# Rows of q and k within SBUF, a third pair of row buffers, the memory update by 136 columns

## The chip, the cores and the metric

The kernel runs on one core of a Trainium2 chip. The metric is device time in microseconds of one execution. The kernel before took 1695.57 us (median of three runs, 1693.65 to 1700.11).

## The reference

Four layers are applied one after another to x, a matrix of 2048 rows and 512 columns: x = x + A(LN(x)), x = x + B(LN(x)), and both once more with the same weights.

A is attention with a compressive memory. The 2048 rows are cut into 4 segments of 512. There are 32 heads of 16 columns. Per head and segment:

```python
logits = qs @ ks.T * scale + causal mask;  p = softmax(logits)
a_dot  = p @ vs
a_mem  = (phi(qs) @ M) / (phi(qs) @ z + 1e-6)      # phi(t) = t + 1 where t > 0, else exp(t)
o      = g * a_mem + (1 - g) * a_dot               # g = sigmoid(beta) of the head
M += phi(ks).T @ vs;   z += sum over rows of phi(ks)
```

The result of all heads is multiplied by wo. B is a Fourier mixing: a = x @ Dre.T and b = x @ Dim.T along the 512 columns, then y = Cre @ a - Cim @ b along the 2048 rows, with given matrices.

## The kernel before, in words

All large products run on TensorE. To keep precision, most operands are split into two f16 numbers, high and low, and a product is three matmuls (high by high, high by low, low by high), collected in PSUM; this is `mm3`. A group is 8 heads of one segment (`NG` = 4 groups per segment, `NGRP` = 32 groups over two layers, numbered in order). Within a group the 8 heads are 2 halves `a` (partitions 0 to 63 and 64 to 127) of 4 heads `p`.

A group goes through these steps, each a generator in the code:

- `s_p` projects q and k of the group (transposed: head columns on partitions, 512 rows along the free axis). `t_split` makes the high and low f16 halves `hl` of each. They have to be spread so that each head's 16 columns lie on partitions of their own, in the row buffers `qst` and `kst`. For this `t_split` stores `hl` to DRAM (2 transfers, tile `d<-w`) and loads it back (4 transfers, `qst<-d` or `kst<-d`): per half, 48 partitions hold high, low, high (q) or high, high, low (k), so that one matmul over 48 partitions does all three products. Two more partitions of `kst` hold a constant (8192) that is written once by `t_ones`; two more of `qst` get the row maxima.
- `s_v` projects v into PSUM, and `t_v` writes it to `vt`. Before, a head pair has three blocks of 16 columns there: v of half 0, ones, v of half 1. So 32 neighbouring columns hold v and ones for either half, and the sums of softmax come out of the same product.
- `s_x` multiplies q by k per 128 rows and takes the maximum of each row with a mask on VectorE (tile `junk`, 32 instructions per group, row maxima `mx`); they are transposed, split and written into `qst` (`qst<-mhl`). Only one group at a time is in this step.
- `s_st` computes the transposed scores, less the maxima, and `t_sel` takes the exponential on ScalarE and the causal selection on POOL (`pt`). After its last matmul the row buffers are free (`("ST", i)`).
- `s_av` multiplies `vt` (as 128 x 32 weights, four column strips of the array) by `pt`.
- `s_mem` multiplies phi(q) by the memory `macc` (segments 1 to 3), and adds the update: phi(k) of 128 rows as weights, all of `vt` of these rows (4 x 48 = 192 columns) as the moving operand, f32, four of them per group; two products with a block mask `bd` on VectorE pick the wanted blocks.
- `s_m`, `t_merge` divide by the sums, add both parts, and split the result for `s_o`, which multiplies by wo, adds x and does the next LayerNorm.

There are `NR` = 2 pairs of row buffers (and 2 of `vt`), used in turn. Group i's rows are loaded once `("ST", i - 2)` is reached. The tile `y` (16 blocks of 512 columns) holds weights at first (`stage`; the value weights in blocks 8 to 11), then the unsplit wd and wo, and later the sums of B.

The order is not written by hand. A planner (`Plan`) steps all generators at build time: every `yield need(engine, tiles)` is a place where it chooses, by its own costs of each instruction, which generator issues next on which engine; a table `LEAN` shifts that choice per step and engine. What comes out is a fixed order on each engine and on SP's queue, from which all transfers are issued. `t_warm` adds matmuls with no use (`onesb`) where the planner expects TensorE to be idle. `tt` puts an elementwise operation on VectorE or POOL. All instructions are recorded under one line, L272, so the profile is read by tile names (`w` are working tiles, `b` PSUM banks).

Of the kernel before, what the change touches and what calls it, by code (L numbers as in the profile page):

```python
# [32 lines left out]
LEAN = dict(s_stT=150.0, s_memV=40.0, s_wV=80.0, s_rY=150.0, t_mergeA=40.0, s_xA=150.0, t_abA=40.0, t_mergeY=-150.0, s_mV=40.0, t_cV=-40.0, s_cA=-80.0, s_oY=40.0, t_cY=80.0, t_lnG=80.0, t_splitV=-40.0, t_phiA=150.0, s_kV=-300.0, t_mergeV=150.0, s_cT=80.0, s_avT=80.0, s_wA=-150.0, t_resV=-150.0, t_selG=40.0, s_lnY=-150.0, t_rowsY=300.0, t_ktY=-80.0)  # L33
# [9 lines left out]
PHM, EARLYLN, FEW = 5, 1, 0  # L43
WARM, IDLE, SPARE = 4200, 500.0, 300.0
DEEP = 1500.0
AHEAD = 2
NR = 2


class Plan:  # L50
# [31 lines left out]
    def key(self, a):  # L82
        f = self.fine.get(a.tensor.name)
        return (a.tensor.name, a.offset // f) if f else a.tensor.name
# [70 lines left out]
    def op(self, eng, name, args, kw):  # L155
# [123 lines left out]
def body(ctx: ExitStack, tc: tile.TileContext, x, wq, wk, wv, wo, beta, wd, cs, out):  # L279
# [61 lines left out]
    vt = [const.tile([128, TT, NP, 3, 16], F32, name=f"vt{i}") for i in range(NR)]  # L341
# [5 lines left out]
    bd = const.tile([128, 2, 4, 32], F32, name="bd")  # L347
# [65 lines left out]
    def share(o, src, s):  # L413
        yield need("A", src, s)
        A.activation(o[:, 0], src, AF.Copy, scale=s)
        A.activation(src, src, AF.Copy, scale=s)
        yield need("VG", o, src)
        tt(o[:, 1], src, o[:, 0], OP.subtract)

# [105 lines left out]
    def t_ones():  # L525
        yield need("G", tag="mz")
        c8 = sb("mz", F16, (32, 128))
        G.memset(c8, 8192.0)
        d8 = tc.dram_tile([2, 2048], F16, name="d8")
        yield gate(("dk", 0))  # L530
        yield need("Y", c8, mode="b")
        Y.dma_start(d8.rearrange("o (p n) -> (o p) n", n=128), c8, est=(609, 341, 172))
        pl.close(c8)
        for i in range(NR):
            for a in range(2):
                yield need("Y", d8, mode="b")
                Y.dma_start(kst[i][64 * a + 48:64 * a + 50].rearrange("r p n -> r (p n)"), d8, est=(415, 341, 472))
        done.add("KR")

    def s_k():  # L540
# [12 lines left out]
        for j in range(NR):  # L553
            V.memset(vt[j][:, :, :, 1, :], 1.0)
        done.add("VI")
        yield need("V")
        bits(rp, 3, 1.0)
        bits(ra, 64, 1.0 / 64)
        cj = sb("en", F32, (128, 2, 4, 32))
# [25 lines left out]
    def t_ln(src, xi, dst, key, direct=False):  # L585
        st = rg("bst", 2, F32, (128, 6))
        V.bn_stats(st, src)
        mv = rg("mv", 6, F32, (128, 4))
        V.bn_aggr(mv[:, 0:2], st)
        yield need("G", mv)  # L590
        rs = rg("rs", 6, F32, (128, 1))
        G.tensor_scalar(mv[:, 2:3], mv[:, 1:2], 1e-5, 2.0 ** -20, op0=OP.add, op1=OP.mult)
        G.tensor_tensor(rs, mv[:, 2:3], mhalf, op=OP.pow)
        G.tensor_scalar(mv[:, 3:4], mv[:, 0:1], rs, -1.0, op0=OP.mult, op1=OP.mult)
# [6 lines left out]
        else:  # L601
            A.activation(hl[:, 0], xi, AF.Copy)
        yield need("VG", xi, hl)
        tt(hl[:, 1], xi, hl[:, 0], OP.subtract)
        pl.close(xi)
        if direct:
# [7 lines left out]
            if pl.free["A"] <= pl.free["V"]:  # L614
# [36 lines left out]
    def t_merge(e, o, gi, g, n, key):  # L651
# [7 lines left out]
        rc = rg("rc", 4, F32, (128, 2, 16))  # L659
        xa = x[:, 0]  # L660

        def view(off, *dims):
            return bass.AP(xa.tensor, xa.offset + off, [list(xa.ap[0])] + [list(d) for d in dims])

        yield need("V", x)
        d = view(16, (496, 2), (32, 16))
        if not gi:
            V.tensor_scalar(rc, d, 1e-6, None, op0=OP.add)
            d = rc
# [4 lines left out]
        for a in range(2):  # L674
            c = slice(16 * a, 16 * a + 16)
            tt(n.rearrange("p (b r) -> p b r", r=32)[:, :, c], view(528 * a, (32, 16), (1, 16)),
# [4 lines left out]
    def t_split(p, key, f, kphi):  # L681
# [10 lines left out]
        done.add(("half", key))  # L692
        yield need("Y", hl)
        d = tc.dram_tile([2, 2, 64, 512], F16)
        for a in range(2):
            Y.dma_start(d[a].rearrange("j p n -> p j n"), hl[64 * a:64 * a + 64], est=(651, 702, 467))
        i = key[1]
        if not kphi or q:
            pl.close(hl)
        elif i >= NR:  # L700
            spawn(t_kt(hl, kphi))
        if i >= NR:
            yield gate(("ST", i - NR))
        yield need("Y", d)
        order = key[0] == "dq"
        dst = (qst if order else kst)[i % NR]
        for a in range(2):
            f = d[a].rearrange("j (d p) n -> (j d) (p n)", p=NP)
            o = dst[64 * a:64 * a + 64].rearrange("r p n -> r (p n)")
            if order:  # L710
# [6 lines left out]
        if kphi and not q and i < NR:  # L717
            yield from t_kt(hl, kphi)
# [41 lines left out]
    def t_v(p, i):  # L760
        yield need("A", p)
        A.activation(vt[i % NR].rearrange("p t j e d -> p (t j) e d")[:, :, 0:3:2, :],
                     p.rearrange("p t (j e d) -> p (t j) e d", j=NP, e=2), AF.Copy, scale=2.0 ** -24)
# [74 lines left out]
    def s_mem():  # L838
        for i in range(NGRP):
# [14 lines left out]
            if s < NSEG - 1:  # L854
# [10 lines left out]
                for a in range(2):  # L865
                    V.tensor_tensor(mu[:, a], mp[:, :, 16 * a:16 * a + 32], bd[:, a], op=OP.mult)
# [28 lines left out]
    def s_x():  # L895
        for i in range(NGRP):
            yield gate(("dq", i), ("dk", i), "CM")
            qs, ks = qst[i % NR], kst[i % NR]
            mx = rg("mx", 2, F32, (128, 2, NP, TT))
# [20 lines left out]
            mhl = rg("mhl", 2, F16, (32, 2, 128))  # L920
# [25 lines left out]
    def s_st():  # L946
        for i in range(NGRP):
            yield gate(("X", i), "KR")
            qs, ks = qst[i % NR], kst[i % NR]
# [143 lines left out]
    def t_c(i, raw, sc, cc):  # L1093
        A.activation(cc[:, 0], raw, AF.Copy, scale=sc)
        A.activation(raw, raw, AF.Copy, scale=sc)
# [8 lines left out]
    def s_c():  # L1104
        k = u = 0
        while u < nunit:
# [18 lines left out]
            gi = gv.bitcast(I32)  # L1125
            V.tensor_scalar(gi, gi, 0x7F800000, None, op0=OP.bitwise_and)
            V.tensor_scalar(csc[:, :m].bitcast(I32), gi, -1.0, float(268 << 23), op0=OP.mult, op1=OP.add)
# [200 lines left out]
```

## Time and profile before

| | |
|---|---|
| runs | 1693.65, 1695.57, 1700.11 us |
| profiled execution | 1699.92 us, its span 1698.2 us |
| mean granted TensorE clock | 0.989 of full speed |
| busy | TensorE 1662.3 us, VectorE 1036.8, ScalarE 872.3, POOL 810.3 |
| matmuls | 11145 records; an f32 matmul leaves two |
| DMA | 222.92 MB, 131 GB/s in the mean |

PE stands for TensorE's matmuls, PEld for its weight loads, DVE for VectorE, ACT for ScalarE, POOL for GpSimd, SPq for the queue of transfers on SyncE. A row of a group shows the operation, the tiles written and read, the size and count, then busy us, the mean ns of one, and the idle time of the engine before them with what ended it. Mean durations of pipelined matmuls overlap; busy time divided by count is what one holds of the engine. In a row of a timeline the first two numbers are start and length in us, and xN is how many instructions are merged.

### The profile page before, as it was taken

How to read it: one execution, taken by the hardware profiler on the slowest of the kernel's cores; microseconds unless marked ns; L12 is line 12 of the kernel's file. 1: busy time of each engine (PE TensorE's matmuls, PEld its weight loads, DVE VectorE, ACT ScalarE, POOL GpSimd, SP SyncE). 2: the span in 40 equal slices, each digit the busy share in tenths (PEclk: the TensorE clock that was granted, in tenths of full speed). 3: DMA queues.
4: the chain of work that ended last, by engine and by line, in shares of the span. 5: the costliest groups of instructions: out<-in, count | busy, mean ns of one | idle time of the engine just before them, and what ended most of it. 6: DMA issues, size and time to landing. Idle time of an engine off the chain costs nothing.

```text
span 1698.2 us, 32247 instructions
## 1 busy us (share of the span) xinstructions
PE 1662.3 (98%) x11145; PEld 734.7 (43%) x11145; DVE 1036.8 (61%) x3262; ACT 872.3 (51%) x1480; POOL 810.3 (48%) x1445
## 2 busy tenths in 40 slices
PE   8889999999999999999999999999999999999999
PEld 4344344444444344444544444443444444444444
DVE  8784865778677786635768558546575765433221
ACT  5487577755656666535376754655455325312000
POOL 4376556575565556634255644635454415322000
PEclk9789999999999999999999999999999999999999
DMA  7546545655357432525746663543435322131423
GB/s 182 147 116 178 128 132 159 172 142 152 94 148 208 126 119 84 189 56 196 193 148 187 182 179 90 132 116 98 140 91 149 105 85 76 57 125 38 143 70 123
DMA packets 208629, 222.92 MB, mean 131 GB/s; under 512 B 104520, under 2 KB 127048, under 8 KB 208464
## 3 DMA queue, kind: packets, MB, share of 16 engines
q1 hardware_dynamic: 208464, 220.85, 45.8%
q8 instruction: 88, 1.44, 0.4%
q14 instruction: 77, 0.63, 0.1%
HBM read 137.40 MB, written 61.87 MB: 117 GB/s over the span
## 4 chain that ended last, share of the span: by engine, by line
PE 77%; DVE 9%; ACT 5%; issue 4%; DMA 3%; POOL 2%; SPq 1%; ACTq 0%; DVEq 0%; POOLq 0%
PE b L272 77%; ACT w L272 4%; DVE junk L272 4%; SPq L272 1%; DVE w L272 1%; POOL w L272 1%; DMA w<-w 1%; DMA w<-x 1%; DVE m L272 1%; DVE mx L272 1%; DVE y L272 1%; DVE bst L272 0%; DVE cam L272 0%; DMA w<-in_cs_dram 0%; DVE pmax L272 0%
## 5 line engine op out<-in xcount | busy, mean ns | idle before, releaser
L272 PEld LDWEIGHTS <-w 128*128 128x128 f16 x5056 | 467.8, 98 | 612.8 <-issue 101.1
L272 PE MATMUL b<-w,w 128*128 128x512 f16 x3072 | 708.5, 380 | 1.7 <-DVE mx L272 0.8
L272 ACT ACTIVATE w<-b,fac 128x512 f32<-128x512 f32 (+1 forms) x728 | 419.2, 655 | 176.3 <-PE b L272 175.8
L272 DVE CUSTOM_DVE_ANT_0 junk<-b,cmask 128x128 bf16<-128x128 f32 (+3 forms) x1024 | 436.3, 483 | 71.6 <-PE b L272 71.1
L272 POOL TENSOR_TENSOR w<-w,w 128x512 f16<-128x512 f32 (+1 forms) x294 | 347.5, 1187 | 247.1 <-ACT w L272 223.6
L272 POOL TENSOR_SCALAR_AFFINE_SELECT w<-w 128x128 f32<-128x128 f32 (+2 forms) x704 | 237.0, 350 | 202.7 <-ACT w L272 194.1
L272 DVE SCALAR_TENSOR_TENSOR y<-b,fyu,y 128x512 f32<-128x512 f32 x200 | 148.9, 745 | 235.6 <-PE b L272 235.2
L272 ACT ACTIVATE w<-w,csc 128x512 f16<-128x512 f32 (+1 forms) x256 | 180.1, 720 | 41.5 <-DVE csc L272 32.8
L272 PE MATMUL b<-g,w 128*128 128x512 f16 x768 | 183.1, 383 | 3.2 <-DMA g<-w 0.8
L272 PE MATMUL b<-wd,w 128*128 128x512 f16 x768 | 176.8, 379 | 0.1
L272 PE MATMUL b<-w,vt 128*32 128x512 f32 (+3 forms) x2048 | 172.4, 449 | 1.9 <-POOL w L272 1.1
L272 ACT ACTIVATE w<-b 128x512 f16<-128x512 f32 x128 | 75.9, 596 | 189.4 <-PE b L272 179.3
L272 DVE SCALAR_TENSOR_TENSOR w<-b,w 128x512 f16<-128x512 f32 x128 | 87.6, 687 | 120.3 <-ACT w L272 118.7
L272 ACT ACTIVATE w<-w 128x512 f16<-128x512 f32 (+1 forms) x137 | 86.5, 632 | 90.1 <-DVE w L272 87.9
L272 PE MATMUL b<-kst,qst 48*128 48x128 f16 (+3 forms) x1024 | 117.5, 304 | 6.3 <-DVE mx L272 3.2
L272 PE MATMUL b<-qst,kst 50*128 50x512 f16 (+3 forms) x1024 | 115.8, 302 | 5.5 <-DVE mx L272 2.2
L272 PE MATMUL b<-w,g 128*128 128x128 f16 x1536 | 96.3, 221 | 0.0
L272 PEld LDWEIGHTS <-g 128*128 128x128 f16 x1536 | 89.6, 99 | 12.7 <-issue 7.8
L272 DVE STREAM_TRANSPOSE m<-b 128x512 f32<-128x512 f32 x112 | 75.6, 698 | 31.1 <-PE b L272 30.7
L272 PEld LDWEIGHTS b<-w,vt 128*32 128x32 f32 x2048 | 54.8, 110 | 87.7 <-issue 48.2
L272 PE MATMUL b<-wo,w 128*128 128x512 f16 x384 | 89.1, 379 | 0.0
L272 PEld LDWEIGHTS <-kst 50*128 50x128 f16 x1024 | 37.3, 94 | 111.7 <-issue 105.2
(105 smaller groups left out, 1019.3 us busy)
## 6 DMA issues: line engine op xcount, KB each, us to landing
w<-in_cs_dram SPq DMA_DIRECT2D x128, 256.0 KB, 3.5
cc<-w SPq DMA_DIRECT2D x128, 256.0 KB, 3.2
w<-cc SPq DMA_DIRECT2D x128, 256.0 KB, 3.1
w<-w SPq DMA_DIRECT2D x96, 256.0 KB, 3.5
d<-w SPq DMA_DIRECT2D x128, 128.0 KB, 2.5
w<-in_x_dram SPq DMA_DIRECT2D x32, 256.0 KB, 3.6
qst<-d SPq DMA_DIRECT2D x64, 128.0 KB, 2.7
kst<-d SPq DMA_DIRECT2D x64, 128.0 KB, 3.3
```

The lines of the kernel that those rows point to most:

```text
L272: r = f(*args, **kw)
```

## The change

- A third pair of row buffers, `kst[2]` and `qst[2]`, is laid over blocks 8 to 11 of y, as f16. Group 2 alone uses it (`ring`); its rows wait until the four value weights have been split (`("W", 2, g)`). Groups from 3 on alternate between pairs 0 and 1; group 3 now waits for group 0, group 4 for group 1, and from group 5 on each for the group two before it, as earlier (`prior`).
- Where the buffer is free when a transfer is planned (groups 0 to 2, and others whose predecessor's step is already planned), `t_split` writes the rows with six transfers from `hl` straight into the row buffer. Otherwise it goes through DRAM as before.
- `vt` is laid out as 16 columns of v and 16 of ones, each with the 8 heads innermost; the host orders the columns of wv so. The update multiplies by the first 17 x 8 = 136 columns; the second attention product takes as weights 32 columns that lie 8 apart. `bd` becomes bf16, and the two products on VectorE read other slices.
- Added waiting points (`YL`, `YB`, `YM`, `YC`, `YS`, all 1) let the planner put other instructions between dependent ones. In the LayerNorms of each layer's first segment (`direct`), two small operations and the low half's subtraction move from POOL to VectorE (`STARTV`); there ScalarE empties PSUM only if it is ahead of VectorE by 300 ns.
- Planner costs for some ScalarE and POOL instructions change, the warming matmuls no longer wait for the mask, and the table `LEAN` has new values. `mx` and `mhl` have one buffer instead of two, `rc` two instead of four. The number of junk tiles stays two.

```diff
-LEAN = dict(s_stT=150.0, ..., t_abA=40.0, ..., s_oY=40.0, t_cY=80.0, t_lnG=80.0, ..., s_cT=80.0, ..., t_ktY=-80.0)
+LEAN = dict(s_stT=150.0, ..., t_abA=150.0, ..., t_cY=80.0, t_lnG=-300.0, ..., s_cT=150.0, ..., s_ldY=300.0, t_lnA=80.0, t_lnY=-40.0, t_abV=300.0, s_oY=40.0, s_oT=150.0, t_phkV=80.0)
+STARTV, YL, YB, YM, YC, YS = 1, 1, 1, 1, 1, 1
+DIRECT = 3
...
+            if name == "activation" and isinstance(kw.get("bias"), bass.AP):
+                c += 80
...
+            if n <= 32:
+                lat = 172
             if name == "tensor_tensor" and kw.get("op") == OP.pow:
-                c = 300 + n * 165
+                c = 290 + n * 165
...
-    vt = [const.tile([128, TT, NP, 3, 16], F32, name=f"vt{i}") for i in range(NR)]
+    kst.append(y[:, 8:10, :].bitcast(F16).rearrange("p a (b n) -> p (a b) n", n=512))
+    qst.append(y[:, 10:12, :].bitcast(F16).rearrange("p a (b n) -> p (a b) n", n=512))
+    ring = [0, 1, 2] + [(i - 3) % 2 for i in range(3, NGRP)]
+    prior = [None] * 3 + [0, 1] + list(range(3, NGRP - 2))
+    vt = [const.tile([128, TT, 32, HG], F32, name=f"vt{i}") for i in range(NR)]
...
-            V.memset(vt[j][:, :, :, 1, :], 1.0)
+            V.memset(vt[j][:, :, 16:, :], 1.0)
...
@@ t_split @@
+        i = key[1]
+        keep = kphi and not q
+        dst = (qst if q else kst)[ring[i]]
         yield need("Y", hl)
+        if i < DIRECT or prior[i] is not None and ("ST", prior[i]) in done:
+            if i == NR:
+                yield gate(*[("W", 2, g) for g in range(NG)])
+            for a in range(2):
+                o = dst[64 * a:64 * a + 64]
+                for r, j in ((0, 0), (16, 1), (32, 0)) if q else ((0, 0), (16, 0), (32, 1)):
+                    yield need("Y", hl)
+                    Y.dma_start(o[r:r + 16], hl[64 * a:64 * a + 64, j], est=(415, 520, 800))
+            done.add(key)
...
+            return
         d = tc.dram_tile([2, 2, 64, 512], F16)
...
-        if i >= NR:
-            yield gate(("ST", i - NR))
+        if i > NR:
+            yield gate(("ST", prior[i]))
...
@@ s_mem @@
-                mp = ps("pj", F32, (128, NP, 48))
+                mp = ps("pj", F32, (128, 17, HG))
                 for t in range(TT):
-                    T.matmul(mp, phk[:, 128 * t:128 * t + 128], v[:, t], start=(t == 0), stop=(t == TT - 1))
+                    T.matmul(mp, phk[:, 128 * t:128 * t + 128], v[:, t, :17], start=(t == 0), stop=(t == TT - 1))
...
-                for a in range(2):
-                    V.tensor_tensor(mu[:, a], mp[:, :, 16 * a:16 * a + 32], bd[:, a], op=OP.mult)
+                for e, d in ((0, HG), (16, 0)):
+                    V.tensor_tensor(view(mu, e, (128, 2), (32, NP), (1, 16)),
+                                    view(mp, HG * e, (NP, 2), (1, NP), (d, 16)),
+                                    view(bd, e, (128, 2), (32, NP), (1, 16)), op=OP.mult)
...
@@ s_av @@
-                                 v[:, t, p].rearrange("k e d -> k (e d)")[:, 16 * a:16 * a + 32], tiles[p][1],
+                                 v[:, t, :, NP * a + p], tiles[p][1],
...
@@ t_ln @@
+        if direct and STARTV:
+            yield need("V", mv)
+            V.tensor_scalar(mv[:, 2:3], mv[:, 1:2], 1e-5, 2.0 ** -20, op0=OP.add, op1=OP.mult)
+            yield need("G", mv)
+            G.tensor_tensor(rs, mv[:, 2:3], mhalf, op=OP.pow)
+            yield need("V", mv, rs)
+            V.tensor_scalar(mv[:, 3:4], mv[:, 0:1], rs, -1.0, op0=OP.mult, op1=OP.mult)
...
-        if "CM" not in done or at - pl.free["T"] < IDLE or pl.lately(at) >= WARM:
+        if at - pl.free["T"] < IDLE or pl.lately(at) >= WARM:
...
-        "wv": f["A_wv"],
+        "wv": f["A_wv"].reshape(D, NG, NP, 2, DH).transpose(0, 1, 4, 3, 2).reshape(D, D),
```

More of the change, by code (lines that the diff above doesn't have):

```diff
@@ L418, in share, with view @@
         tt(o[:, 1], src, o[:, 0], OP.subtract)
+    def view(t, off, *dims):
+        return bass.AP(t.tensor, t.offset + off, [list(t.ap[0])] + [list(d) for d in dims])
     def flat(t):
@@ L601, in t_ln @@
         else:
+            if YL:
+                yield need("A", xi)
             A.activation(hl[:, 0], xi, AF.Copy)
-        yield need("VG", xi, hl)
-        tt(hl[:, 1], xi, hl[:, 0], OP.subtract)
+        if direct:
+            yield need("V", xi, hl)
+            V.tensor_tensor(hl[:, 1], xi, hl[:, 0], op=OP.subtract)
+        else:
+            yield need("VG", xi, hl)
+            tt(hl[:, 1], xi, hl[:, 0], OP.subtract)
         pl.close(xi)
@@ L658, in t_merge @@
         pl.close(e, o)
[L659 to L663, printed above, removed]
+        rc = rg("rc", 2, F32, (128, 2, 16))
         yield need("V", x)
-        d = view(16, (496, 2), (32, 16))
+        d = view(x, 16, (512, 2), (32, 16))
         if not gi:
             V.tensor_scalar(rc, d, 1e-6, None, op0=OP.add)
+            if YM:
+                yield need("V", rc)
             d = rc
@@ L692, in t_split @@
         done.add(("half", key))
+        i = key[1]
+        keep = kphi and not q
+        dst = (qst if q else kst)[ring[i]]
         yield need("Y", hl)
+        if i < DIRECT or prior[i] is not None and ("ST", prior[i]) in done:
+            if i == NR:
+                yield gate(*[("W", 2, g) for g in range(NG)])
+            for a in range(2):
[4 more added lines that the diff above has]
+            done.add(key)
+            if keep:
+                yield from t_kt(hl, kphi)
+            else:
+                pl.close(hl)
+            return
         d = tc.dram_tile([2, 2, 64, 512], F16)
@@ L696, in t_split @@
             Y.dma_start(d[a].rearrange("j p n -> p j n"), hl[64 * a:64 * a + 64], est=(651, 702, 467))
-        i = key[1]
-        if not kphi or q:
+        if keep:
+            spawn(t_kt(hl, kphi))
+        else:
             pl.close(hl)
-        elif i >= NR:
-            spawn(t_kt(hl, kphi))
-        if i >= NR:
-            yield gate(("ST", i - NR))
+        if i > NR:
+            yield gate(("ST", prior[i]))
         yield need("Y", d)
-        order = key[0] == "dq"
-        dst = (qst if order else kst)[i % NR]
         for a in range(2):
@@ L897, in s_x @@
             yield gate(("dq", i), ("dk", i), "CM")
[L898 to L899 removed]
+            qs, ks = qst[ring[i]], kst[ring[i]]
+            mx = rg("mx", 1, F32, (128, 2, NP, TT))
             left = [0]
@@ L947, in s_st @@
         for i in range(NGRP):
-            yield gate(("X", i), "KR")
-            qs, ks = qst[i % NR], kst[i % NR]
+            yield gate(("X", i), ("KR", ring[i]))
+            qs, ks = qst[ring[i]], kst[ring[i]]
             kt = scores("t")
```

51 lines of the change are left out of this document (34 added, 17 removed).

## The prediction

> **What bounds the kernel now.** I read the page first: span, busy time by engine and the chain that ended last.
>
> ```profile
> span 1698.2 us, 32247 instructions
> ...
> PE 1662.3 (98%) x11145; PEld 734.7 (43%) x11145; DVE 1036.8 (61%) x3262; ACT 872.3 (51%) x1480; POOL 810.3 (48%) x1445
> ...
> PE 77%; DVE 9%; ACT 5%; issue 4%; DMA 3%; POOL 2%; SPq 1%; ACTq 0%; DVEq 0%; POOLq 0%
> ```
>
> TensorE is busy for 98% of the span and holds 77% of the chain; only 1698.2 - 1662.3 = 35.9 us are free of it. But a busy matmul may be a slow one, so the second view was the busy time by stretch. Its columns are the stretch, its length, busy us of each engine with the instructions begun, and the granted clock.
>
> ```profile
> core 0: us, PE busy (x) PEld busy (x) DVE busy (x) ACT busy (x) POOL busy (x), PEclk, DMA share, GB/s
> ...
> 20.00:40.00 20.00, 19.50 (x176) 11.29 (x174) 18.38 (x73) 13.79 (x24) 8.10 (x7) 1.00 0.58 145
> 40.00:60.00 20.00, 16.59 (x82) 5.84 (x81) 20.00 (x81) 6.73 (x12) 6.16 (x7) 0.94 0.84 253
> 60.00:70.00 10.00, 8.18 (x29) 2.02 (x28) 9.18 (x32) 5.23 (x10) 3.11 (x11) 0.50 0.01 2
> 70.00:80.00 10.00, 9.79 (x42) 3.09 (x42) 3.23 (x11) 4.61 (x10) 3.66 (x6) 0.76 0.46 107
> 80.00:90.00 10.00, 9.86 (x120) 6.39 (x120) 5.16 (x18) 9.12 (x17) 8.29 (x16) 1.00 0.76 146
> 90.00:100.00 10.00, 8.79 (x73) 3.69 (x74) 8.04 (x42) 9.97 (x20) 8.40 (x19) 0.94 0.64 173
> 100.00:120.00 20.00, 17.85 (x157) 9.18 (x148) 16.92 (x74) 14.56 (x25) 14.86 (x25) 0.78 0.40 107
> 120.00:140.00 20.00, 17.44 (x122) 5.24 (x122) 11.56 (x37) 18.39 (x34) 14.42 (x31) 0.83 0.27 70
> 140.00:160.00 20.00, 19.57 (x150) 8.11 (x150) 6.46 (x12) 18.22 (x33) 13.72 (x27) 1.00 0.78 223
> ...
> 200.00:700.00 500.00, 496.38 (x3520) 214.77 (x3519) 352.24 (x1084) 325.45 (x553) 303.65 (x525) 1.00 0.49 138
> 700.00:900.00 200.00, 196.41 (x1211) 91.24 (x1210) 116.36 (x343) 105.23 (x168) 90.83 (x129) 0.99 0.54 161
> 900.00:1500.00 600.00, 595.12 (x4245) 260.98 (x4243) 367.99 (x1207) 300.35 (x525) 289.64 (x571) 1.00 0.43 117
> ...
> 1600.00:1650.00 50.00, 50.00 (x233) 22.70 (x232) 12.02 (x16) 0.00 (x0) 0.00 (x0) 1.00 0.34 116
> ```
>
> There are two regimes. From 200 us on TensorE sets the pace: 496 of 500 and 595 of 600 us. Between 40 and 140 us it does not: few matmuls begin, and the clock falls to 0.50 in one stretch and 0.76 to 0.83 in others. There the attention of the first four groups sets the pace, one after another, since nothing else is ready before the first segment's output exists. The third view asks where the row maxima of the scores (32 per group, on VectorE, tile junk) lie; the fourth takes the row transfers of the third group, numbered 2, from the timeline of SP's queue, beside the last score matmuls of group 0 and the last split of a value weight.
>
> ```profile
> core 0: us, DVE busy (x), PEclk, DMA share, GB/s
> 34.00:50.00 16.00, 13.28 (x32) 1.00 0.94 255
> 50.00:70.00 20.00, 13.63 (x32) 0.69 0.33 115
> 70.00:90.00 20.00, 0.00 (x0) 0.88 0.61 127
> 90.00:110.00 20.00, 13.48 (x32) 0.80 0.53 133
> ```
>
> ```profile
> 72.97 2.63 SPq L272 DMA_DIRECT2D d<-w  x4
> ...
> 83.43 1.74 SPq L272 DMA_DIRECT2D qst<-d  x4
> 85.21 1.81 SPq L272 DMA_DIRECT2D kst<-d  x4
> ```
>
> ```profile
> 83.01 0.40 PE L272 MATMUL b<-qst,kst 50*128 50x128 f16 x8
> ```
>
> ```profile
> 59.01 1.16 POOL L272 TENSOR_TENSOR w<-y,w 128x512 f16<-128x512 f32 x1 [0.21 <-ACT y L272]
> ```
>
> Groups 0 and 1 take their maxima until 70 us, then none is taken for 20 us, and group 2 follows from 90. Its rows were stored to DRAM by 72.97 + 2.63 = 75.6 us, but loaded only at 83.43, the moment the last matmul on group 0's buffers ended (83.01 + 0.40 = 83.41). So one hole at the start is a wait for a buffer.
>
> **The change, part by part.** *Third pair of row buffers.* Group 2 gets rows of its own, in a part of y that held the value weights; they are free once the last value weight is split, at 59.01 + 1.16 = 60.2 us, well before 73. The load need no longer wait for 83.41. With q and k split at 73, twelve issues at the 2.63 / 4 = 0.66 us of the store row make 7.9 us at most, and with a landing the maxima of group 2 can start at 79 to 83 instead of 90. Group 3, which waited for group 1's buffers, now waits for group 0's, so it follows group 2 directly. From group 5 on the buffer waited for is the same as before. The new wait of group 2's rows on the value weights' split sits on SP's queue; the next segment's inputs and the transposes for its LayerNorm stand behind it there, and they are wanted only when the projections of segment 1 begin. What can be won is bounded by nothing at all (ScalarE, 14.56 + 18.39 + 18.22 = 51.2 of 60 us busy from 100 to 160, paces the rest anyway) and by the whole hole of 20 us. I take what VectorE was idle in the hole, 6.8 us of 70:80 and 4.8 us of 80:90, together -12 us (0 to -20). What is late next is ScalarE's exponentials.
>
> *Direct transfers.* Where the buffer is free when the transfer is planned, the two stores and four loads of a q or k become six transfers within SBUF; the issues on SP's queue stay six. In steady state a group's rows wait for a buffer, as group 2's did, so the old way stays and nothing is won. Groups 0 to 2 and the first of layer 2 profit.
>
> ```profile
> d<-w SPq DMA_DIRECT2D x128, 128.0 KB, 2.5
> ...
> kst<-d SPq DMA_DIRECT2D x64, 128.0 KB, 3.3
> ...
> qst<-mhl SPq DMA_DIRECT2D x128, 4.0 KB, 1.7
> ```
>
> The store and the load took 2.5 + 3.3 us to land. A transfer within SBUF of 64 KB is not in the trace: the one of 4 KB took 1.7 us, and I let it cost up to the 3.3 of the load. That saves 2.5 to 4.1 us of latency. At group 0 VectorE has only 20 - 18.38 = 1.6 us free in 20:40 to use it: -1.5 us (0 to -3). At layer 2's start TensorE is idle for 200 - 196.41 = 3.6 us in 700:900: -1 us (0 to -2.5).
>
> *Update by 136 columns.* The memory update multiplies phi(k) with 17 x 8 = 136 columns of values and ones in place of 192.
>
> ```profile
> L272 PE MATMUL b<-w,g 128*128 128x128 f16 x1536 | 96.3, 221 | 0.0
> L272 PEld LDWEIGHTS <-g 128*128 128x128 f16 x1536 | 89.6, 99 | 12.7 <-issue 7.8 <-DVE fac L272 0.2
> ...
> L272 PE MATMUL b<-vt,w 128*128 128x192 f32 x192 | 38.6, 338 | 1.4 <-ACT vt L272 1.2 <-POOL w L272 0.2
> ...
> L272 PEld LDWEIGHTS b<-vt,w 128*128 128x128 f32 x192 | 30.9, 190 | 10.7 <-issue 2.7 <-DVE mx L272 2.3 <-ACT vt L272 1.6
> ```
>
> 192 records hold TensorE for 38.6 us. If all of it goes with the columns, 38.6 x 56 / 192 = 11.3 us are saved; if the weight load of 190 ns binds, nothing. In the nearest row, the projections of v, loads of 99 ns stand before matmuls that hold TensorE for 96.3 / 1536 = 63 ns each, so a load longer than its matmul is mostly hidden; I take -8 us (0 to -11). They lie on TensorE, which is the bound in most of the span. VectorE's two products per update keep their count and size.
>
> *Values with the head innermost.* The price of that is the weight of the second attention product: 32 values side by side become 32 values eight apart.
>
> ```profile
> L272 PEld LDWEIGHTS b<-w,vt 128*32 128x32 f32 x2048 | 54.8, 110 | 87.7 <-issue 48.2 <-POOL w L272 23.4 <-DVE mx L272 3.0
> ```
>
> ```profile
> L272 PE MATMUL b<-w,vt 128*32 128x128 f32 x512 | 21.4, 280 | 0.7 <-POOL w L272 0.5
> ```
>
> No load of the trace is strided. Four loads go side by side, so 2048 make 512 passes. Lower end: no cost. Upper end: the strided 32 columns cost what 128 do in one row, 190 in place of 110 ns, and all 80 ns of every pass are exposed: 512 x 0.08 = 41 us. Since the loads are issued ahead of matmuls of 280 ns and more, I take it close to the lower end: 27 ns (a third of the 80) exposed in the 128 passes of the shortest matmuls, 3.5 us, rounded to +3. [...]
>
> *The rest.* The added waiting points and the planner's new costs issue no instruction, and one buffer less for mx, mhl and rc binds nothing, because the next group's scores are planned after the transpose that reads mx. Should it bind, VectorE's maxima would queue behind it. In the first LayerNorms a subtraction and two small operations per tile move from POOL to VectorE; VectorE has 1.6 us free there, so I count 0 (1.5 either way). The new table reorders everything and I cannot derive its order. Its reach: the matmuls with 512 f16 columns.
>
> ```profile
> L272 PE MATMUL b<-w,w 128*128 128x512 f16 x3072 | 708.5, 380 | 1.7 <-DVE mx L272 0.8 <-ACT w L272 0.4
> ...
> L272 PE MATMUL b<-g,w 128*128 128x512 f16 x768 | 183.1, 383 | 3.2 <-DMA g<-w 0.8 <-ACT w L272 0.7 <-ACT g L272 0.7
> ...
> L272 PE MATMUL b<-wd,w 128*128 128x512 f16 x768 | 176.8, 379 | 0.1
> ...
> L272 PE MATMUL b<-wo,w 128*128 128x512 f16 x384 | 89.1, 379 | 0.0
> ```
>
> They hold TensorE for 1157.5 us; at the pace of 1600:1650, 50 / 233 = 0.2146 us each, the 4992 would take 1071 us. A table can move some of these 86 us, either way. I count 0 in the sum and 17 us (a fifth, my choice) as a rival in each direction.
>
> **The sum.** -12 - 1.5 - 1 - 8 + 3 = -19.5 us. The profiled execution took 1699.92 us, its span and 1.7 us around it, so 1680.4; it lies 4.35 us above the median of 1695.57, so against the median the forecast is 1676 us.
>
> **The rivals.** *ScalarE paces the start anyway.* For it: 51.2 of 60 us busy from 100 to 160, and 9.97 of 10 in 90:100. Against: 5.2, 4.6 of 10 us in the stretches before, where the earlier work would go. The start is then worth nothing, only -8 + 3 remain: 1691 us. The same comes out if the third pair does not do what it says, because the planner still sends group 2's rows late.
>
> *The table fills the gaps, or opens them.* 17 us less than the forecast is 1659; 17 us more, 1693. For it: 86 us of gaps. Against: TensorE waits visibly only 3.6 of 500 us from 200 to 700, so no single wait can be named that it removes.
>
> *The strided weights stall TensorE: slower.* Place: every pass of the second attention product, where the load stands between two matmuls of the same array columns. The price is the full 41 us in place of 3: 1676 + 38 = 1714. It decides from (19.5 + 3) / 512 = 44 ns exposed per pass, where it eats the whole gain. Against: four loads run beside each other, and 54.8 us busy for 2048 loads of 110 ns says that most of a load is latency that overlaps.
>
> **How the numbers follow.** Forecast 0.55, ScalarE or an idle third pair 0.18, a better table 0.13, a worse one 0.06, strided weights 0.08. The likeliest case alone spans 1660 to 1690: the start from 0 to -20 and the update from 0 to -11, not both at an end. The range 1655 to 1699 takes in all but the last case and half of the tail of the better table. About 0.5%, 8.5 us, is what a measurement of this kernel tells from no change. Faster by more, under 1687: nearly all of the forecast, the better table and a part of the second case, 0.72. Within: most of the second case and the worse table, 0.18. Slower: the strided weights and a little of the worse table, 0.10.
>
> **What would show it.** In the changed kernel's windows the 32 maxima of group 2 begin before 84 us, and those of group 3 before 105. The row b<-vt,w has 136 columns and under 33 us. The load row b<-w,vt stays near 110 ns and the busy time of its matmuls of 128 columns near 21.4 us; 190 ns and twice the busy time would mean the slower case. Stretches after 200 us hold as many matmuls per us as now, or the table has moved them. The prediction is wrong if the clock in 40:140 stays as low with the hole closed, for then the start was not paced by buffers.

## The result and the profile after

The changed kernel takes 1719.47 us (median of four runs, 1711.94 to 1720.61) against 1696.17 us of the kernel before on the same chip: a ratio of 1.0127, with a 95% interval of 1.0111 to 1.0143. It is slower by 23 us; the forecast was 1676 us, and the time lies beyond the range. The profiled execution took 1719.67 us.

The page of the changed kernel, with its span, busy times, shares of the chain and two rows of the transfers:

```profile
span 1717.9 us, 32388 instructions
...
PE 1664.3 (97%) x11160; PEld 742.7 (43%) x11160; DVE 1042.8 (61%) x3290; ACT 862.8 (50%) x1478; POOL 796.9 (46%) x1419
...
PE 77%; DVE 8%; issue 4%; DMA 4%; ACT 3%; POOL 2%; SPq 2%; DVEq 0%; ACTq 0%; POOLq 0%
...
kst<-w SPq DMA_DIRECT2D x120, 64.0 KB, 2.6
qst<-w SPq DMA_DIRECT2D x108, 64.0 KB, 2.9
```

Nothing here looks like a new bound. TensorE is still 97% busy and the chain has nearly the same shares. What changed is small in every line: TensorE is idle for 1717.9 - 1664.3 = 53.6 us in place of 35.9. That is 17.7 of the 19.7 us by which the span grew. The last two rows hold the surprise, to which we come below.

Where the idle time lies is told by the stretches of the changed kernel:

```profile
core 0: us, PE busy (x) PEld busy (x) DVE busy (x) ACT busy (x) POOL busy (x), PEclk, DMA share, GB/s
0.00:200.00 200.00, 171.17 (x1231) 77.39 (x1235) 145.28 (x533) 125.39 (x214) 104.05 (x193) 0.90 0.47 132
200.00:700.00 500.00, 490.40 (x3502) 214.45 (x3495) 352.69 (x1115) 318.07 (x546) 297.31 (x516) 1.00 0.45 128
700.00:1500.00 800.00, 788.46 (x5441) 353.93 (x5440) 487.87 (x1560) 401.94 (x691) 371.18 (x678) 1.00 0.43 125
```

The two stretches of the kernel before that the prediction does not show in this form:

```profile
0.00:200.00 200.00, 180.08 (x1276) 79.88 (x1276) 153.10 (x564) 129.49 (x219) 114.00 (x205) 0.91 0.58 155
...
700.00:1500.00 800.00, 791.52 (x5454) 352.22 (x5453) 484.35 (x1549) 405.58 (x691) 380.47 (x700) 1.00 0.46 128
```

TensorE's idle time in the three stretches is 28.8, 9.6 and 11.5 us after, against 19.9, 3.6 and 8.5 us before. So half of the added idle time arises in the first 200 us, which the change was expected to shorten, and half in the steady part, where the prediction expected a gain.

The maxima of the changed kernel (tile junk), by stretches cut at the groups:

```profile
core 0: us, DVE busy (x), PEclk, DMA share, GB/s
34.00:49.00 15.00, 0.02 (x1) 1.00 0.45 121
49.00:69.00 20.00, 13.62 (x32) 0.83 0.71 227
69.00:93.00 24.00, 13.75 (x32) 0.86 0.51 138
93.00:98.00 5.00, 0.00 (x0) 1.00 0.92 218
98.00:115.00 17.00, 13.49 (x32) 0.90 0.34 103
```

The hole of some 20 us between groups 1 and 2 is down to about 6 us, so the third pair does what it was said to do. But group 0 begins at 49 us, where it began at 35 us before, group 1 at 72 where it began at 51, and group 2 at 98.6 where it began at 91.

The products that use the values, by shape, in the changed kernel:

```profile
L280 PE MATMUL b<-vt,w 128*128 128x136 f32 x192 | 28.9, 290 | 3.0 <-ACT vt L280 0.9 <-DVE m L280 0.8 <-POOL w L280 0.8
...
L280 PE MATMUL b<-w,vt 128*32 128x128 f32 x512 | 22.9, 287 | 1.0 <-POOL w L280 0.7
```

```profile
L280 PEld LDWEIGHTS b<-w,vt 128*32 128x32 f32 x2048 | 67.7, 145 | 82.7 <-issue 47.8
```

The update holds TensorE for 28.9 us in place of 38.6, and a strided load takes 145 ns in place of 110. TensorE's busy time as a whole is 2.0 us longer all the same; among what grew are the warming matmuls (tile onesb), 28.4 us against 23.5.

### The profile page after: what moved, and what is told of

It reads as the page before. It is cut to its first block, busy times and chain, and to the rows that moved or that the text cites. A ratio compares the mean times of both kernels' runs of the same rounds, so it can differ in the third digit from the quotient of the medians.

```text
span 1717.9 us, 32388 instructions
## 1 busy us (share of the span) xinstructions
PE 1664.3 (97%) x11160; PEld 742.7 (43%) x11160; DVE 1042.8 (61%) x3290; ACT 862.8 (50%) x1478; POOL 796.9 (46%) x1419
## 4 chain that ended last, share of the span: by engine, by line
PE 77%; DVE 8%; issue 4%; DMA 4%; ACT 3%; POOL 2%; SPq 2%; DVEq 0%; ACTq 0%; POOLq 0%
PE b L280 77%; DVE junk L280 3%; ACT w L280 3%; DMA w<-w 2%; SPq L280 2%; POOL w L280 2%; DVE w L280 1%; DVE mx L280 1%; DMA w<-in_x_dram 1%; DVE m L280 0%; DVE y L280 0%; DVE cam L280 0%; DVE bst L280 0%; DVE pmax L280 0%; DMA qst<-w 0%
## 5 line engine op out<-in xcount | busy, mean ns | idle before, releaser
L280 POOL TENSOR_TENSOR w<-w,w 128x512 f16<-128x512 f32 (+1 forms) x285 | 336.4, 1188 | 189.7 <-ACT w L280 175.9
L280 ACT ACTIVATE w<-w,csc 128x512 f16<-128x512 f32 (+1 forms) x256 | 174.2, 725 | 29.1 <-DVE csc L280 25.1
L280 PE MATMUL b<-qst,kst 50*128 50x512 f16 (+1 forms) x992 | 112.7, 301 | 11.4 <-ACT w L280 5.9
L280 PE MATMUL b<-kst,qst 48*128 48x128 f16 (+1 forms) x992 | 111.1, 302 | 5.5 <-DVE mx L280 2.9
L280 PEld LDWEIGHTS b<-w,vt 128*32 128x32 f32 x2048 | 67.7, 145 | 82.7 <-issue 47.8
L280 DVE TENSOR_REDUCE cam<-w 128x1 bf16<-128x512 f32 x128 | 82.0, 677 | 16.9 <-DMA w<-in_cs_dram 16.6
L280 DVE STREAM_TRANSPOSE m<-b 128x512 f32<-128x512 f32 x112 | 76.2, 699 | 19.9 <-PE b L280 17.4
```

Of the source, the lines that this page charges most:

```text
L280: r = f(*args, **kw)
```

## The experiments

The question was which part costs the time. Five theories stood: the new order by itself (O), the strided weights (W), the direct transfers' time on SP's queue (D), the late start by the waiting points (S), and the bytes of the direct transfers (B).

**The parts alone, in the order of before.** The first kernel takes only the layout with the head innermost (with the bf16 mask and the fewer buffers for mx, mhl and rc), the second also the 136 columns, both with every queue's order as it was.

```diff
 s1_stride
+    vt = [const.tile([128, TT, 32, HG], F32, name=f"vt{i}") for i in range(NR)]
+    T.matmul(mp, phk[:, 128 * t:128 * t + 128], v[:, t, :24], ...)      # still 192 columns
+    v[:, t, :, NP * a + p]                                              # strided weights of s_av
+    "wv": f["A_wv"].reshape(D, NG, NP, 2, DH).transpose(0, 1, 4, 3, 2).reshape(D, D),
 s2_update, on top of it
-    T.matmul(mp, ..., v[:, t, :24], ...)
+    T.matmul(mp[:, :17], ..., v[:, t, :17], ...)                        # 136 columns
```

> The kernel before with its order of instructions on every engine kept, and only the layout of the values changed: head innermost, so the second attention product loads weights 8 apart; the memory update still multiplies 192 columns. Theory O (the order): the loss of the changed kernel lies in the new order of the work and not in its edits, so this one costs 0 to 5 us over the kernel before; the load row rises from 110 to about 145 ns and the excess of these matmuls by some 4 us. Theory W (strided weights, the rival of the prediction): 20 us or more over the kernel before. Theory D (direct row transfers): as O, 0 to 5 us.

> As s1_stride, same order of instructions, and the update multiplies 136 columns. O: the row of the update falls from 38.6 to about 29 us as in the changed kernel, so 10 us less than s1_stride, 5 to 10 us under the kernel before. W: still 10 us or more over the kernel before. D: as O.

The layout alone takes 1698.59 us against 1696.72, a ratio of 1.0012 (1.0003 to 1.0022); with 136 columns 1695.75 us, 0.9996 (0.9986 to 1.0005). The weight loads of the first, and the update of the second:

```profile
L273 PEld LDWEIGHTS b<-w,vt 128*32 128x32 f32 x2048 | 69.3, 144 | 79.0 <-issue 45.7 <-POOL w L273 21.5 <-DVE mx L273 2.4
```

```profile
L273 PE MATMUL b<-vt,w 128*128 128x136 f32 x192 | 29.6, 291 | 1.2 <-ACT vt L273 1.0
```

2048 loads, each 34 ns longer, cost 2 us (0.5 to 3.7 by the interval): W falls as the cause of 23 us. The narrower update frees 38.6 - 29.6 = 9.0 us of TensorE's busy time, yet the kernel gains only 1698.59 - 1695.75 = 2.8 us. The span falls by no more, 1695.7 to 1693.2 us, and the other rows of matmuls became 5.7 us longer together, 4.6 of them in the scores (tiles qst and kst); the granted clock was 0.990 in the mean of the profiled execution, against 0.993. Why they became longer was not followed. An engine that is 98% busy did not hand on here all that was taken off it.

**The direct transfers alone, in the order of before.**

```diff
 s3_direct, in t_split
+        if i < NR or ("ST", i - NR) in done:
+            six  Y.dma_start(o[r:r + 16], hl[64 * a:64 * a + 64, j])   # where the stores stood
+        else:
             the two stores, and later the four loads
```

> The kernel before with its order kept, and rows of q and k moved within SBUF at the place of the store wherever the buffer is planned to be free then (two pairs of buffers, not three). O: within 3 us of the kernel before, since what waits for the rows keeps its place in every queue. W: no difference. D: each direct transfer holds the queue of SP for 0.59 us where a load took 0.43, and what stands behind is late: 10 to 20 us over the kernel before.

1732.60 us, a ratio of 1.0207 (1.0193 to 1.0221). The direction is D's, but 36 us are more than it had said, and where the rest arises was not followed. SP's queue in this kernel, around 275 us:

```profile
272.47 3.86 SPq L273 DMA_DIRECT2D qst<-w  x6
276.44 3.74 SPq L273 DMA_DIRECT2D kst<-w  x6
280.62 1.29 SPq L273 DMA_TRANSPOSE w<-w  x1
```

The same place in the kernel before:

```profile
268.94 2.73 SPq L272 DMA_DIRECT2D d<-w  x4
271.76 1.31 SPq L272 DMA_TRANSPOSE w<-w  x1
```

The DMA_TRANSPOSE turns k for phi(k). Before, four stores of 2.73 us together stood ahead of it; the loads came later, behind it. Now twelve transfers of 3.86 + 3.74 = 7.6 us stand ahead of it, and it is issued 8.15 us after the first of them in place of 2.82, so 5.3 us later. The rows of 36 of the 64 sets (a set is a q or a k of one group) reach their buffer without DRAM, and the kernel loses.

**Parts taken out of the changed kernel, its order kept.** In s4 the values have their old layout and the update its 192 columns. In s5 only two of a q's or k's six direct transfers are issued from group 3 on, and in s9 all six with half of the columns each; these two leave rows stale, so they tell of time alone.

```diff
 s4_oldvalues
+    vt = [const.tile([128, TT, NP, 3, 16], F32, name=f"vt{i}") for i in range(NR)]
+    T.matmul(mp, ..., v[:, t], ...)                                     # 192 columns, contiguous weights
 s5_third
+    if i < DIRECT or r == 0:
         Y.dma_start(o[r:r + 16], hl[64 * a:64 * a + 64, j], ...)
 s9_half
+    if i < DIRECT:
         Y.dma_start(o[r:r + 16], hl[64 * a:64 * a + 64, j], ...)
+    else:
+        Y.dma_start(o[r:r + 16, :, :256], hl[64 * a:64 * a + 64, j, :256], ...)
```

> The changed kernel with its order kept, and the old layout of the values and the update by 192 columns put back. O: the update's 10 us come back and the strided loads' 4 us go: 1723 to 1728 us, slower than the changed kernel. W: 1690 to 1700 us, as the stall goes. D: as O.

1717.36 us, 1.0123 (1.0105 to 1.0141): 2 us less than the changed kernel, where O and D had expected more time and W 1690 to 1700 us. In the new order the two edits on the values together are worth nothing, or cost 2 us. The loads are back at 110 ns.

> The changed kernel with its order kept; of the six direct transfers of a q or k only two are issued from group 3 on, so the other rows keep what an earlier group left there (the scores of these groups are computed from rows that are partly old; all other work is the same). It takes 0.59 us of SP's queue per transfer left out. Theory D (the issue time of the direct transfers makes SP's queue late, and all that stands behind it): 1700 to 1710 us, 10 to 20 us less than the changed kernel. Theory O (the new order itself, with whatever transfers): 1717 to 1720 us.

1703.75 us, 1.0052 (1.0033 to 1.0071): without two thirds of these transfers about 16 of the 23 us are gone, as D had said.

> The changed kernel with its order kept and every transfer still issued, but from group 3 on each direct transfer moves only half of its columns (the other half of the rows stays from an earlier group; nothing else is left out). Theory D in its narrow form (what costs is the time that SP's queue needs to issue 12 transfers before the transpose of k behind them): 1716 to 1721 us, as the changed kernel. Rival B (the bytes, that is the landing of the rows or the load on the DMA engines): 1706 to 1713 us, half or more of the way to s5_third's 1703.75.

1721.58 us, 1.0154 (1.0139 to 1.0169), level with the changed kernel. Its issues of k's rows, and the landing of those with half the bytes:

```profile
L281 SPq DMA_DIRECT2D kst<-w x120: 546/591/652, 38.9 to 1321.9; - x120
```

```profile
kst<-w SPq DMA_DIRECT2D x108, 32.0 KB, 2.0
```

Half the bytes land in 2.0 us in place of 2.6, and the kernel gains nothing; an issue still takes 591 ns in the median. So B falls, and with it a late landing of the rows: what counts is the number of issues. What one issue costs, from the tile kst of the changed kernel (count, then shortest, median and longest in ns):

```profile
L280 SPq DMA_DIRECT2D kst<-w x120: 546/592/1077, 39.0 to 1319.4; - x120
L280 SPq DMA_DIRECT2D kst<-d x48: 245/418/966, 63.8 to 1416.0; - x48
```

A direct transfer holds SP's queue for 592 ns, a load from DRAM for 418. The planner counts 415 for either, so the twelve of a q and a k are through 12 x 0.18 = 2.1 us later than it believes. (s5 takes out eight of the twelve, 4.7 us, and so more than this error: its 16 us are no measure of the wrong price alone.) The chain from there to TensorE can be followed at one place. SP's queue of the changed kernel:

```profile
1065.20 1.93 SPq L280 DMA_DIRECT2D qst<-w  x3
1067.18 0.57 SPq L280 DMA_DIRECT2D w<-w  x1
1067.85 1.82 SPq L280 DMA_DIRECT2D qst<-w  x3
1069.72 3.80 SPq L280 DMA_DIRECT2D kst<-w  x6
1073.61 1.27 SPq L280 DMA_TRANSPOSE w<-w  x1
```

The same instructions in s5, with a third of the transfers:

```profile
1050.53 0.60 SPq L280 DMA_DIRECT2D qst<-w  x1
1051.18 0.58 SPq L280 DMA_DIRECT2D w<-w  x1
1051.85 0.59 SPq L280 DMA_DIRECT2D qst<-w  x1
1052.49 1.23 SPq L280 DMA_DIRECT2D kst<-w  x2
1053.83 2.45 SPq L280 DMA_TRANSPOSE w<-w  x1
```

From the first of q to the transpose it is 8.4 us in the one and 3.3 us in the other. Then, in the changed kernel, the timelines of POOL, ScalarE and TensorE, one row each:

```profile
1076.78 1.15 POOL L280 TENSOR_TENSOR w<-w 128x512 f32<-128x512 f16 x1 [3.79 <-DMA w<-w]
```

```profile
1077.97 0.72 ACT L280 ACTIVATE w<-w,fac 128x512 f32<-128x512 f32 x1 [4.85 <-POOL w L280]
```

```profile
1080.88 0.79 PE L280 MATMUL b<-qst,kst 50*128 50x384 f16 x3 [1.35 <-ACT w L280]
```

POOL adds the halves of k when the transposed k lands, ScalarE waits 4.85 us to begin phi(k), and the exponentials that are to empty PSUM stand behind phi(k) in ScalarE's fixed order. So the score matmuls find no free bank and TensorE waits 1.35 us. In s5, ScalarE's wait at the same instruction is this:

```profile
1060.51 0.72 ACT L280 ACTIVATE w<-w,fac 128x512 f32<-128x512 f32 x1 [1.03 <-POOL w L280]
```

One such place costs TensorE 1.5 us at most in the changed kernel, the longest wait of the second row below, and no page shows it as a bound. TensorE's waits for ScalarE's working tiles over the whole kernel (sum, count, longest) before, after, and in s5:

```profile
PE b L272 <- ACT w L272: 5.1, 13, 0.9
```

```profile
PE b L280 <- ACT w L280: 12.6, 23, 1.5
```

```profile
PE b L280 <- ACT w L280: 8.3, 17, 1.6
```

So this wait is 7.5 of the 17.7 us of added idle time, and 4.3 of the 9.2 us of idle time that s5 takes away (53.6 - 44.4). Most of the rest of what s5 wins lies in TensorE's waits for VectorE (mx from 10.3 to 7.7 us, w from 4.8 to 1.8), which were not followed back to the queue. Nor does a late ScalarE cost time by itself: it stands idle ahead of this step of phi(k) for 37.3 us in the changed kernel, 14.8 before and 19.2 in s5, but also for 34.9 us in s11 below, the fastest kernel of all, whose TensorE waits for it for 1.2 us at most. At the place above it costs, since the next matmuls of TensorE stand behind it. No run moved the transpose alone in the changed kernel's order.

The stretches of s5 show which part of the loss the transfers make:

```profile
0.00:200.00 200.00, 170.54 (x1235) 76.96 (x1239) 145.66 (x534) 125.49 (x214) 104.73 (x193) 0.91 0.46 131
200.00:700.00 500.00, 494.91 (x3533) 217.80 (x3526) 356.28 (x1123) 321.52 (x552) 302.22 (x521) 1.00 0.43 124
700.00:1500.00 800.00, 794.04 (x5485) 357.17 (x5484) 493.24 (x1565) 403.82 (x694) 376.94 (x687) 1.00 0.41 118
```

TensorE idles 5.1 and 6.0 us in the steady stretches, where it was 9.6 and 11.5, and 3.6 and 8.5 before. The idle time added in the steady part is that of the transfers. The first 200 us still have 29.5 us of idle time: that half has another cause.

**Parts taken out, the planner ordering anew.** In these the order of everything changes with the part, and the table `LEAN` is still the one fitted to the changed kernel, its values chosen for that program.

```diff
 s6_gate, in s_k
-        yield gate(("F", 1))
 s7_nodirect, in t_split: all rows through DRAM, the third pair kept
-        if i < DIRECT or prior[i] is not None and ("ST", prior[i]) in done:
+        if False:
 s8_noyields
-STARTV, YL, YB, YM, YC, YS = 1, 1, 1, 1, 1, 1
+STARTV, YL, YB, YM, YC, YS = 0, 0, 0, 0, 0, 0
```

> The changed kernel without one of its added waiting points: the constants of the step s_k (bits, the sigmoid of beta, the block mask) are again planned from the start and not only after the second group's weight factors. Theory S (the start is late because the added waiting points and the table put small work ahead of group 0's projections): the first maxima fall from 49 to about 44 us, and the end to 1712 to 1718 us. O and D: the first maxima may move, the end stays within 1715 to 1730, since the rest is ordered anew and as dense as before.

1723.36 us, 1.0154 (1.0119 to 1.0188). The maxima of group 0 begin at 40.3 us in place of 49.0, and the end comes no earlier, where S had expected 1712 to 1718 us. TensorE is still idle for 27.3 of the first 200 us.

> The changed kernel, ordered anew, with all rows through DRAM and the third pair kept. D: faster than the changed kernel, 1705 to 1712 us, although the rows of group 0 land some us later. O: slower, 1725 to 1735, since the table was made for another program.

1716.36 us, 1.0126 (1.0104 to 1.0148). This lies between what D and O had said and decides nothing by its time: with the transfers gone, the planner made another order with a table that was not fitted to it. But its first maxima begin at 48.3 us, as late as in the changed kernel, so the late start does not need the direct transfers.

> The changed kernel, ordered anew, with all added waiting points that have a switch off, and the small LayerNorm operations back on POOL. S: the first maxima at 44 to 46 us and the end 1712 to 1720. O: 1720 to 1730 us, the order without the points the table was made for. D: 1715 to 1725 us, as the direct transfers stay.

1716.57 us, 1.0126 (1.0107 to 1.0146), with the first maxima at 42.4 us. `STARTV` = 0 also takes the small LayerNorm operations back to POOL. S and D had both allowed this time, so it does not decide between them; but the start is earlier by some 7 us, the end by some 3 us, which the intervals do not tell from nothing, and 26.9 of the first 200 us are still idle. With s6, S falls as the cause of the 23 us: an earlier group 0 does not bring an earlier end.

**All edits, with the right price.** If the planner's price is the fault and not the edits, the same edits with an issue counted at 600 ns, and the table fitted to that, should win the loss back.

```diff
 s10_priced, in t_split
-    Y.dma_start(o[r:r + 16], ..., est=(415, 520, 800))
+    Y.dma_start(o[r:r + 16], ..., est=(600, 520, 800))
-LEAN = dict(..., t_lnG=-300.0, ..., s_wA=-150.0, ..., s_ldY=300.0, ..., t_phkV=80.0)
+LEAN = dict(..., t_lnG=80.0, ..., s_wA=80.0, ..., s_ldY=150.0, ..., t_ktY=-80.0, ..., t_phkV=-150.0)
```

> The changed kernel with all its edits, but the planner counts a direct transfer's issue with 600 ns instead of 415, near the 590 measured, and the table is fitted to that price; the step s_k's added waiting point stays. D: the transposes of k no longer come later than planned; 1693 to 1700 us, level with the kernel before. O (any order with the added waiting points and a fitted table does badly): 1710 us or more.

1694.67 us, 0.9991 (0.9980 to 1.0002): level with the kernel before, and 25 us faster than the change as it was made. Its stretches, and its TensorE's waits for ScalarE:

```profile
0.00:200.00 200.00, 180.76 (x1322) 81.46 (x1323) 155.74 (x590) 132.81 (x227) 110.37 (x202) 0.94 0.54 144
```

```profile
PE b L280 <- ACT w L280: 2.2, 6, 0.9
```

It still writes 126 of k's transfers directly, each still near 0.59 us; the wait for ScalarE is 2.2 us in place of 12.6, and the idle time of the first 200 us is 19.2 us in place of 28.8. Both halves of the loss are gone with price and table, while the edits stay, so these transfers do not cost 23 us in every order. They may still cost something: s11 below, which leaves them out from group 3 on and changes more besides, is 9.5 us faster. Whether the price or the table repaired it isn't told apart, in the start or after it: they were changed together, and no run fits a table at the old price of 415.

**What is left of a gain.** The last two kernels keep the direct way for groups 0 to 2 alone. s11 also leaves the small LayerNorm operations on POOL; s12 leaves them on VectorE and issues the transpose of k ahead of its row transfers. Both drop the waiting point that s6 dropped.

```diff
 s11_first3
-        if i < DIRECT or prior[i] is not None and ("ST", prior[i]) in done:
+        if i < DIRECT:
-STARTV, ... = 1, ...
+STARTV, ... = 0, ...
 s12_ktfirst, with STARTV = 1: in t_split, ahead of the six transfers
+            if keep:
+                kt = sb("kt", F16, (128, 2, 512))
+                Y.dma_start(kt..., hl..., transpose=True)
 both: est=(600, 520, 800), a table LEAN of their own
-        yield gate(("F", 1))
```

> Third pair and update by 136 columns kept; direct transfers for the first three groups alone, priced at 600 ns; the small LayerNorm operations back on POOL, s_k's waiting point taken out, and a table fitted to this. D: 1680 to 1690 us, faster than both kernels. O: 1700 us or more.

1685.13 us, 0.9939 (0.9921 to 0.9957): faster than both kernels, by 0.6% in the case of the one before. Its page and its stretches:

```profile
span 1680.0 us, 32413 instructions
...
PE 1646.4 (98%) x11178; PEld 741.9 (44%) x11178; DVE 1041.3 (62%) x3275; ACT 865.1 (51%) x1480; POOL 796.5 (47%) x1432
```

```profile
0.00:200.00 200.00, 177.19 (x1329) 81.92 (x1330) 152.66 (x536) 131.74 (x226) 111.46 (x204) 0.98 0.55 153
200.00:700.00 500.00, 498.41 (x3550) 221.69 (x3549) 360.05 (x1137) 327.09 (x560) 305.92 (x526) 1.00 0.49 143
```

TensorE idles 1.6 us from 200 to 700 and is busy for 1646.4 us in all, 16 us less than before, with 1329 instead of 1276 matmul records in the first 200 us.

> As s11_first3, but the small LayerNorm operations stay on VectorE, and in the first three groups the transpose of k is issued ahead of the six transfers of its rows; own fitted table. D: 1683 to 1693 us. O: 1700 us or more.

1691.33 us, 0.9971 (0.9955 to 0.9987): with the transpose first, too, the kernel is a little faster than the one before, but slower than s11. The two kernels differ in their tables and in the place of the LayerNorm operations as well, so the 6 us between them have no single cause that was shown.

## Why the prediction was wrong

**The step that failed** is the one on direct transfers: "the issues on SP's queue stay six. In steady state a group's rows wait for a buffer, as group 2's did, so the old way stays and nothing is won." Both halves misled. The old way did not stay: the planner found the buffer free for 40 of the 64 sets, six transfers each, by the 120 + 108 of the page's two rows and 12 more into group 2's buffers (tile y); 34 of the 40 belong to groups from 3 on. And six is the right count, but not of the same thing in the same place. Before, two stores stood ahead of the transpose of k and four loads behind it; now all six stand ahead, at 0.59 us each, where 0.42 was planned. The prediction had the row that bounds this, the store's 0.66 us, and used it for group 2 alone. It also did not name what is queued behind these issues in the steady state, the transpose of k, nor who waits for that. The term was put at -2.5 us together, with nothing for the steady state; taking out two thirds of these transfers from group 3 on was worth 16 us, and the edit alone in the old order cost 36.

**The start**, -12 us, was right in mechanism and wrong in sum. The maxima of group 2 follow those of group 1 closely (98.6 after 92.8), as the third pair should bring about. But the step "in the first LayerNorms ... I count 0 (1.5 either way)" and the table's 0 were not: group 0 began 14 us later, group 2 at 98.6 where the prediction wanted less than 84, and group 3 at 121 where it wanted less than 105. s10 has the same edits with the maxima of group 0 from 35.3 us and those of group 2 from 87.5, so the lateness was made by the order and not by the third pair, the waiting points or VectorE's extra work as such. The idle time in the first 200 us (29.5 us in s5 against 19.9) is large enough for the 7.6 us by which s5 is still above the kernel before. But s6 and s8 moved the start forward without moving the end much, so this half is attributed and not shown, and what in the order makes it stays open. The clock, granted at 0.83 from 40 to 140 us before, was 0.87 there after: a small rise, from one profile each, where the prediction had named a clock that stays as low as a sign against it.

**The update**, -8 us: right as a row (28.9 us, under the 33 that were named), wrong as a time. 9.0 us of busy time gave 2.8 us in the old order. The term took TensorE's busy time for its path, with an order that was made for the old update.

**The strided weights**, +3 us: right. They cost 2 us in the old order. The load row did rise from 110 to 145 ns, which the prediction had called a sign of the slower case, but the busy time of the short matmuls rose from 21.4 to 22.9 us only. The 35 ns that a load takes longer are small in the kernel's time; that the loads run ahead of their matmuls is the author's guess at the reason, and was not tested by itself.

**The rivals.** ScalarE pacing the start would have given 1691 us. The case against it named the stretches with 5.2 and 4.6 of 10 us and left out the one from 80 to 90, with 9.12. TensorE did come to wait for ScalarE, 12.6 us in place of 5.1, but at the place that was followed it was through ScalarE's order behind a late transpose, in the steady stretch. The table that opens gaps, at 1693 us, came nearest in kind: the gaps of TensorE grew by 17.7 us. It had no place in the prediction, only an amount, and it was counted from a forecast that held two gains which were not there. The rival on the slower side, the strided weights, was the wrong one. A better one stood in the diff: the price that the planner puts on a new transfer within SBUF, 415, beside a store row of 660 ns and the transfers `qst<-mhl` of the kernel before, also within SBUF, which took 580 ns in the median and for which the kernel's own code counts 609.

## What to carry to other kernels

A transfer that saves a trip through DRAM still costs its issue, here 592 ns of the queue, and in a fixed order on one queue what stands behind it pays: count the issues that come to stand ahead of each transfer on the queue, and name who waits for that transfer. When a planner or a hand-made order assumes a duration for a new instruction, compare it with the nearest row of the trace first. Here an error of 0.18 us, repeated twelve at a time, lay in an order whose gaps no share of busy time showed; right price and new table together won 25 us back. And do not count time taken off an engine that is 98% busy as time of the kernel: here 9.0 us gave 2.8.

## What the runs showed of the hardware

- The issue of a 64-KB transfer within SBUF, from 64 partitions to 16, held SP's queue for 592 ns in the median (120 of them), that of a 4-KB transfer within SBUF (`qst<-mhl`) for 580 ns, that of a load from DRAM into the rows for 418 ns. With half the bytes in s9 the issue took 591 ns, the landing 2.0 us in place of 2.6, and the kernel's time did not fall (1721.58 against 1719.47 us). The full transfer's landing took 2.6 to 2.9 us in the median, no less than the store's 2.5 and little less than the loads' 2.7 to 3.3 us in the kernel before.
- f32 weights of 32 columns that lie eight values apart load in 144 to 145 ns in place of 110, and 2048 such loads cost the kernel 2 us (s1).
- The granted clock in the first 200 us was 0.98 in s11 against 0.91 before, at about the same busy time of TensorE (177 and 180 us) and with more matmuls begun (1329 against 1276), in one profiled execution of each.
